# A 2-D Fourier transform with a channel mix: rows n and -n added on VectorE before the first products

## The chip, the core and the metric

The kernel runs on one core of one Trainium2 chip. The metric is device time in microseconds (us), the median over runs. The engines are named as in the profile: PE is TensorE with its weight loads (PEld), DVE is VectorE, ACT is ScalarE, POOL is GpSimd, SP is SyncE. PE writes only to PSUM; a result there is brought to SBUF by an "eviction" on ACT or DVE.

## What is computed

The input `x` is 8 x 3072 x 256 (batch, sequence, feature). The reference transforms both the sequence and the feature axis, keeps the real part, and feeds it to a channel mix:

```python
X = np.fft.fft(np.fft.fft(x, axis=1), axis=2).real
x_prev = np.concatenate([np.zeros((B, 1, D)), X[:, :-1, :]], axis=1)
xk = mu_k * X + (1.0 - mu_k) * x_prev
xr = mu_r * X + (1.0 - mu_r) * x_prev
k = np.maximum(xk @ w_k, 0.0)          # w_k: 256 x 1024
v = k * k @ w_v                        # w_v: 1024 x 256
out = v / (1.0 + np.exp(-(xr @ w_r)))  # w_r: 256 x 256
```

The input is real and only the real part is kept. So row n with feature f and row -n with feature -f (indices modulo 3072 and 256) enter with the same cosine. Their sum is all that the transform needs.

## The kernel before, in words

Each of the 8 batches goes through three product stages of the transform and then through the channel mix.

- **Loading.** `load_rows` (L105) brings 96 partitions of 16 rows into a tile `xh`, twice per batch (h = 0, 1). The upper 48 partitions hold the rows mirrored against the lower 48. The transfer is issued from POOL and turns float32 into float16.
- **Feature halves.** `butterfly` (L128) makes the sum and the difference of the two feature halves on DVE: four instructions of 96x2048 per batch, result `eo`.
- **Stage a.** `a_item` (L392): 8 products of 104 columns and one eviction of 128x832 on ACT, 8 items per batch. Where no `eo` is made (all of batch 0, half of batch 1) `a_sum` (L404) takes both feature halves as two accumulated products of 208 columns each, for 4 rows at a time.
- **Stage d.** `d_units` (L420), called by `d_item` and `d_half`: four products of 63 to 65 columns for each of 13 units; the eviction writes `g_all`. Its table is `w_eo`.
- **Stage c.** `c_item` (L446): two products of 64 columns for each of 27 slices, from `g_all` and the table `m_c` (for slice 0 also `mn`); the eviction writes `pq`. Then DVE forms `halves`, `diff` and the mixes (L466 to L526).
- **Channel mix.** 48 chunks of 512 rows, four steps each. `k_piece` (L543) is four products of 512 columns and a Relu eviction of 128x1024 on ACT, `square` (L552) squares on DVE, `v_tile` (L569) is 8 products of 256 columns, `r_item` (L557) is 8 products of 256 columns once per chunk, `v_out` (L580) scales on DVE and SP writes out.

**What sets the order.** Every engine runs its instructions in the order in which the program writes them; `pin_order` (L91) fixes that. The work of the transform for batch b+2 is put by hand at numbered steps of batch b with `at(step, function, ...)` (L626 to L727): kind "x" runs between `k_piece` and `v_tile`, kind "w" behind `v_tile`. Batch 0 runs ahead of step 0 (L598 to L620), batch 1 in steps 4 to 19. PSUM has three slots of 1024 columns (`ps_w`) and two of 512 (`ps_v`). `keep_busy` (L151) issues products with zeros that nobody reads.

**Tables at the start.** POOL fills index tables and, at L189 to L200, the angles `ueo` of the table `w_eo`. DVE wraps the angles at L272, ahead of the row tables (L284 to L295), of the angles of `m_c` (L341 and L342) and of everything that it does to batch 0:

```python
    ts(ueo, ueo, TURN - 1, ALU.bitwise_and)
    par_i = const.tile([P, 1], INT32)
    ts(par_i, pcol_i, 1, ALU.bitwise_and)
...
    m_angles(0, NJ1)
    m_wrap(0, NJ1)
```

`m_sine` (L328) turns the angles into the table on ACT, `m_first` (L334) mends its slice 0 with ACT and one DVE memset.

Of the kernel before, what the change touches and what calls it, by code (L numbers as in the profile page):

```python
# [9 lines left out]
FP32 = mybir.dt.float32  # L10
# [29 lines left out]
def kernel(  # L40
# [14 lines left out]
    P = 128  # L55
# [6 lines left out]
    xh_pool = ctx.enter_context(tc.tile_pool(name="xh", bufs=3))  # L62
# [39 lines left out]
    xh_t = {}  # L102
    eo_t = {}

    def load_rows(b, h, g, q0, nq):  # L105


        q = 16 * h + q0
        r = (64 - q if q else 32) if g else q
        src = dataclasses.replace(x[b, r:r + 1, :],  # L110
                                  ap=[[64 * D, N1], [-D if g else D, nq], [1, D]])
        nc.gpsimd.dma_start(out=xh_t[b, h][48 * g:48 * g + 48, q0:q0 + nq], in_=src)  # L112

    def load_part(b, h, q0, nq):
        load_rows(b, h, 0, q0, nq)
        if h == 0 and q0 == 0:
            load_rows(b, h, 1, 1, nq - 1)
            load_rows(b, h, 1, 0, 1)
        else:
            load_rows(b, h, 1, q0, nq)  # L120

    def load_xh(b, h):
        xh_t[b, h] = xh_pool.tile([96, 16, 256], FP16, name="xh")
        load_part(b, h, 0, 16)

    V = nc.vector

    def butterfly(b, h, e):  # L128
        if e == 0:
            eo_t[b, h] = eo_pool.tile([96, 16, 2, 128], FP16, name="eo")  # L130
        xh = xh_t[b, h]
        V.tensor_tensor(out=eo_t[b, h][:, :, e], in0=xh[:, :, 0:128], in1=xh[:, :, 128:256],  # L132
                        op=ALU.subtract if e else ALU.add)
# [46 lines left out]
    for h in range(2):  # L180
        xh_t[0, h] = xh_pool.tile([96, 16, 256], FP16, name="xh")
    load_rows(0, 0, 0, 0, 8)
# [4 lines left out]
    load_rows(0, 0, 1, 1, 7)  # L187
    load_rows(0, 0, 1, 0, 1)
# [9 lines left out]
    for c in range(2):  # L198
        nc.gpsimd.tensor_scalar(out=ueo[:, :, c], in0=veo_i[:, :, c], scalar1=pd_f,  # L199
                                scalar2=0.75 * (1 - c) * TURN, op0=ALU.mult, op1=ALU.add)  # L200
    load_part(0, 0, 8, 8)


    kst_i = const.tile([P, NJ + 64], INT32)
    nc.gpsimd.iota(kst_i[0:64, 0:NJ], pattern=[[2, NJ]], base=0, channel_multiplier=0)
    nc.gpsimd.iota(kst_i[64:128, 0:NJ], pattern=[[2, NJ]], base=-1, channel_multiplier=0)
    nc.gpsimd.iota(kst_i[:, NJ:NJ + 64], pattern=[[1, 64]], base=0, channel_multiplier=0)
    load_part(0, 1, 0, 8)
    load_part(0, 1, 8, 8)

# [9 lines left out]
    m_c = const.tile([P, 2 * NJ, 64], FP16)  # L220
    mn = const.tile([P, 64], FP16)
    V.memset(m_c, 0.0)
    V.memset(mn, 0.0)
# [20 lines left out]
    ts(one["p"], pcol_i, TURN / 48.0, MUL)  # L244
    ts(one["g"], pcol_i, 48.0, ALU.is_ge)
    ts(one["t"], one["p"], -2.0, MUL, 47.0 * TURN / 48.0, ADD)
    ts(one["n"], one["t"], one["g"], MUL, one["p"], ADD)
    ts(one["o0"], one["g"], 0.5 * TURN, MUL, 0.5 * TURN, ADD)
    ts(one["o1"], one["g"], 0.5 * TURN, MUL, 0.75 * TURN, ADD)
    for part, c, ph in ((0, 0, 0.75 * TURN), (0, 1, 0.0), (1, 0, one["o0"]), (1, 1, one["o1"])):  # L250
        ts(u_w[:, 0, part, :, c], k1c_i, one["n"], MUL, ph, ADD)
    ts(one["ph"], one["p"], TURN / 96.0, ADD)
    ts(one["a"], pcol_f, 48.0, ALU.is_lt, one["p"], MUL)
    ts(one["b"], pcol_f, 48.0, ALU.is_ge, one["ph"], MUL)
    ts(one["fa"], one["g"], -0.25 * TURN, MUL, 0.75 * TURN, ADD)
    ts(one["fb"], one["g"], 0.25 * TURN, MUL, 0.5 * TURN, ADD)
    for part, c, by, ph in ((0, 0, "a", one["fa"]), (0, 1, "b", one["fb"]),
                            (1, 0, "a", 0.5 * TURN), (1, 1, "b", 0.5 * TURN)):
        ts(u_w[:, 1, part, :, c], k1c_i, one[by], MUL, ph, ADD)
    u_f = u_w.rearrange("p t a k c -> p (t a k c)")  # L260
    ts(u_f, u_f, TURN - 1, ALU.bitwise_and)
    nc.scalar.activation(out=w_pm[:, :, 0:2],
                         in_=_v(u_f, 0, [(4 * NU, 2), (0, 2), (1, 4 * NU)]), func=AF.Sin,
                         bias=m_pi, scale=TWO_PI / TURN)
    nc.scalar.activation(out=w_pm[:, :, 2], in_=_v(u_f, 0, [(4 * NU, 2), (1, 4 * NU)]),
                         func=AF.Sin, bias=p_pi, scale=-TWO_PI / TURN)

    for i in range(2):
# [11 lines left out]
    ast = const.tile([P, NJ + 64], FP32)  # L280
    ast_i = const.tile([P, 64], INT32)
    row = {n: const.tile([P, 1], FP32, name=f"row_{n}")
           for n in ("s", "c", "rr", "rs", "ph0", "ph", "sgn")}
# [3 lines left out]
    ts(row["rr"], t64_i, row["c"], ADD, row["s"], ADD)  # L287
    ts(row["rs"], t64_i, row["c"], ADD, float(TURN) / S, MUL)
    ts(row["ph0"], row["c"], 0.25 / 32 * TURN, MUL, 0.75 * TURN, ADD)
    ts(row["ph"], row["s"], 0.25 / 32 * TURN, MUL, row["ph0"], ADD)  # L290
    ts(row["sgn"], row["s"], 1.0 / 16, MUL, -1.0, ADD)
    ts(ast_i, kst_i[:, NJ:NJ + 64], row["rr"], MUL, float(TURN) / R, MUL)
    ts(ast_i, ast_i, TURN - 1, ALU.bitwise_and)
    V.tensor_copy(out=ast[:, NJ:NJ + 64], in_=ast_i)
    ts(ast[:, 0:NJ], kst_i[:, 0:NJ], row["rs"], MUL, row["ph"], ADD)  # L295
# [3 lines left out]
    def rows():  # L299
# [17 lines left out]
           .rearrange("p a b -> p (a b)").bitcast(INT32)[:, 0:NJ * 64]  # L317
           .rearrange("p (s t) -> p s t", t=64))
    lo64, hi64 = slice(0, 64), slice(64, 128)

    def m_angles(j0, j1):
        V.tensor_tensor(out=ang[:, j0:j1], in0=_v(ast, j0, [(1, j1 - j0), (0, 64)]),
                        in1=_v(ast, NJ, [(0, j1 - j0), (1, 64)]), op=ALU.add)

    def m_wrap(j0, j1):
        ts(ang[:, j0:j1], ang[:, j0:j1], TURN - 1, ALU.bitwise_and)

    def m_sine(j0, j1):  # L328
        for part, odd in ((hi64, 0), (lo64, 1)):
            nc.scalar.activation(  # L330
                out=m_c.rearrange("p (j o) t -> p j o t", o=2)[part, j0:j1, odd],
                in_=ang[part, j0:j1], func=AF.Sin, bias=m_pi[part], scale=TWO_PI / TURN)

    def m_first():  # L334

        im = slice(96, 128)
        nc.scalar.activation(out=m_c[im, 0], in_=m_c[im, 0], func=AF.Copy, scale=row["sgn"][im])
        V.memset(m_c[hi64, 0, 0:1], 0.0)
        nc.scalar.activation(out=mn[hi64], in_=m_c[hi64, 0], func=AF.Copy, scale=-1.0)

    m_angles(0, NJ1)  # L341
    m_wrap(0, NJ1)  # L342

    def gather(dst, w, n):
        nc.gpsimd.indirect_dma_start(dst, None, w,
                                     bass.IndirectOffsetOnAxis(ap=row_i[:, n:n + 1], axis=0))

    xh_t[1, 0] = xh_pool.tile([96, 16, 256], FP16, name="xh")

    def loads():  # L350
        load_part(1, 0, 0, 8)
        for a in range(2):
            next(row_part)
            gather(wk_sb[0][a], moe_w_k, a)
        nc.gpsimd.dma_start(out=wv_sb, in_=moe_w_v.rearrange("(fc p) v -> p fc v", p=128))
        load_part(1, 0, 8, 8)
        for a in range(2):
            gather(wr_sb[0][a], moe_w_r, a)
# [30 lines left out]
    def a_tile(b):  # L389
        a_t[b] = y_pool.tile([P, 2, 2, NU, 64], FP16, name="a")  # L390

    def a_item(b, h, e, j, eng="A"):  # L392

        if (h, e, j) == (0, 0, 0):
            a_tile(b)
        eo = eo_t[b, h]
        ps = ps_w()
        for i in range(8):
            nc.tensor.matmul(out=ps[:, 128 * i:128 * i + 4 * NU], lhsT=eo[:, 8 * j + i, e, :],  # L399
                             rhs=w_pm[0:96, int(h + j + i == 0), 0], start=True, stop=True)  # L400
        evac(_v(a_t[b], 128 * NU * e + 16 * h + 8 * j, [(32, 4 * NU), (1, 8)]),
             _v(ps, 0, [(1, 4 * NU), (128, 8)]), eng)

    def a_sum(b, h, q0, eng="A", n=4):  # L404
# [4 lines left out]
        xh = xh_t[b, h]  # L409
        ps = ps_w() if n == 4 else ps_v()  # L410
        for i in range(n):
            for k in range(2):
                nc.tensor.matmul(out=ps[:, 256 * i:256 * i + 8 * NU],  # L413
                                 lhsT=xh[:, q0 + i, 128 * k:128 * k + 128],
                                 rhs=w_pm[0:96, int(h + q0 + i == 0), k:k + 2],
                                 start=(k == 0), stop=(k == 1))
        evac(_v(a_t[b], 16 * h + q0, [(32, 8 * NU), (1, n)]),
             _v(ps, 0, [(1, 8 * NU), (256, n)]), eng)
# [360 lines left out]
```

## Time and profile before

| | us |
|---|---|
| median of 3 runs (453.25 to 454.44) | 453.86 |
| span of the profiled execution, first to last instruction | 450.4 |
| PE busy in the span | 439.9 |
| DVE busy | 352.6 |
| ACT busy | 345.0 |
| POOL busy | 43.5 |

The profiled execution has a span of 450.4 us; no total of its own is recorded beside it, and the median of the runs lies 3.46 us above the span.

How to read it: a timeline line gives the start in us, the duration in us, the engine, the source line, the operation, what it writes and reads, and how many instructions are merged (x16). Durations of PE products contain their way through the array and overlap, so the cost of a product in a stream is taken from start to start of neighbouring groups. A row of windows gives, after the stretch and its length, the busy time of PE, PEld, DVE, ACT and POOL with the instructions of each, then the granted TensorE clock as a share of full speed, the DMA share and GB/s. A group row gives the count, the total and the mean ns of one.

### The profile page before, as it was taken

To read this page: it belongs to the slowest core of one execution; us is meant where nothing else is said; L and a number is where in the kernel's file an instruction comes from. 1 tells how busy PE (TensorE), PEld (TensorE's weight loads), DVE (VectorE), ACT (ScalarE), POOL (GpSimd) and SP (SyncE) were. 2 spreads that over 40 slices of the span, in tenths; PEclk is the share of its full clock that TensorE was granted. 3 is DMA by queue.
4 is the path that set the end of the run, shared out by engine and by line. 5 is a ranking of instruction groups with operands and counts; after the bars stand their busy time and mean duration, and the time that the engine had idled before them with its cause. 6 is when DMAs were issued, how large, how long until landed. Compare 5 with 4: busy or idle time off the path is not lost.

```text
span 450.4 us, 9677 instructions
## 1 busy us (share of the span) xinstructions
PE 439.9 (98%) x4073; PEld 321.4 (71%) x4073; DVE 352.6 (78%) x472; ACT 345.0 (77%) x390; POOL 43.5 (10%) x78
## 2 busy tenths in 40 slices
PE   7899999999999999999999999999999999999996
PEld 4667777777777777777777777777777777676764
DVE  6599969986788878977789877888779755997453
ACT  6599898787878778877888778887778787666661
POOL 8862010102000110001100010000000000000000
PEclk8799999999999999999999999999999999999999
DMA  7997961737622385225923272222323232233333
GB/s 103 159 201 109 180 119 47 141 71 129 131 49 69 60 158 109 54 60 98 172 48 71 51 137 67 53 66 54 72 48 72 47 71 58 61 71 71 72 70 95
DMA packets 43856, 40.22 MB, mean 89 GB/s; under 512 B 3986, under 2 KB 42388, under 8 KB 43188
## 3 DMA queue, kind: packets, MB, share of 16 engines
q1 hardware_dynamic: 27524, 25.05, 22.7%
q0 software_dynamic: 16128, 14.42, 22.5%
q8 instruction: 32, 0.52, 0.5%
q10 hardware_dynamic: 160, 0.13, 0.1%
q14 instruction: 12, 0.10, 0.1%
HBM read 28.84 MB, written 25.17 MB: 120 GB/s over the span
## 4 chain that ended last, share of the span: by engine, by line
PE 93%; ACT 2%; POOL 1%; DMA 1%; DVE 1%; issue 0%; POOLq 0%
PE psV L576 37%; PE psW L538 36%; PE psW L562 9%; PE psW L399 4%; PE psW L457 3%; PE psW L427 2%; PE psW L413 1%; ACT rl L548 1%; DMA xh<-in_x_dram 1%; POOL xh L112 1%; ACT L567 0%; PE psV L413 0%; ACT r L567 0%; DVE y L474 0%; POOL ueo L199 0%
## 5 line engine op out<-in xcount | busy, mean ns | idle before, releaser
L548 ACT ACTIVATE rl<-psW 128x1024 f16<-128x1024 f32 x192 | 196.2, 1024 | 87.7 <-PE psW L538 87.5
L576 PE MATMUL psV<-wv_sb,k 128*128 128x256 f16 x1536 | 198.7, 272 | 0.0
L538 PE MATMUL psW<-x,wk 128*128 128x512 f16 (+1 forms) x776 | 196.7, 377 | 0.8 <-DVE x L518 0.5
L555 DVE TENSOR_TENSOR k<-rl 128x2048 f16<-128x2048 f16 (+1 forms) x98 | 117.5, 1202 | 60.7 <-ACT rl L548 60.0
L576 PEld LDWEIGHTS <-k 128*128 128x128 f16 x1536 | 143.6, 98 | 23.0 <-DVE k L555 0.2
L538 PEld LDWEIGHTS <-wk 128*128 128x128 f16 x776 | 75.8, 98 | 50.9 <-issue 1.3
L586 DVE SCALAR_TENSOR_TENSOR o<-psV,r 128x512 f32<-128x512 f32 (+1 forms) x97 | 66.1, 683 | 20.8 <-PE psV L576 19.2
L507 DVE TENSOR_TENSOR x<-y,t 128x1536 f16<-128x1536 f16 x60 | 57.5, 959 | 2.1
L387 ACT ACTIVATE a<-psW 128x832 f16<-128x832 f32 x61 | 52.3, 859 | 3.6 <-PE psW L413 3.6
L562 PE MATMUL psW<-wr,x 128*128 128x256 f16 x384 | 49.8, 273 | 0.0
L567 ACT ACTIVATE r<-psW 128x1024 f16<-128x1024 f32 x48 | 48.9, 1018 | 0.8 <-PE psW L562 0.8
L112 POOL DMA_DIRECT2D xh<-in_x_dram x46 | 28.7, 632 | 215.2 <-DVE eo L132 214.3
L562 PEld LDWEIGHTS <-x 128*128 128x128 f16 x384 | 37.6, 98 | 14.4
L399 PEld LDWEIGHTS <-eo 96*128 96x128 f16 x416 | 24.4, 97 | 11.6
L132 DVE TENSOR_TENSOR eo<-xh 96x2048 f16<-96x2048 f16 x26 | 31.5, 1214 | 0.0
L387 ACT ACTIVATE pq<-psW 128x896 f16<-128x896 f32 (+5 forms) x34 | 28.5, 845 | 1.1 <-PE psW L457 1.1
L399 PE MATMUL psW<-w_pm,eo 96*128 96x104 f16 x416 | 27.6, 209 | 0.0
L387 ACT ACTIVATE g_all<-psW 128x1024 f16<-128x1024 f32 (+1 forms) x31 | 26.4, 857 | 0.0
L457 PEld LDWEIGHTS <-g_all 128*128 128x128 f16 x432 | 16.8, 98 | 8.5 <-ACT g_all L387 2.3
L427 PEld LDWEIGHTS <-a 128*128 128x128 f16 x416 | 16.6, 97 | 7.2 <-issue 0.4
L494 DVE TENSOR_SCALAR t<-d,mu_m 128x1536 f16<-128x1536 f16 x32 | 19.7, 614 | 0.0
L474 DVE TENSOR_TENSOR y<-pq 128x896 f16<-128x896 f16 (+5 forms) x38 | 18.6, 532 | 1.0 <-ACT pq L387 0.7
(100 smaller groups left out, 154.7 us busy)
## 6 DMA issues: line engine op xcount, KB each, us to landing
out_dram<-o SPq DMA_DIRECT2D x190, 128.0 KB, 2.4
xh<-in_x_dram POOLq DMA_DIRECT2D x20, 384.0 KB, 6.5
xh<-in_x_dram POOLq DMA_DIRECT2D x6, 360.0 KB, 7.8
xh<-in_x_dram POOLq DMA_DIRECT2D x10, 192.0 KB, 5.3
wv_sb<-in_moe_w_v_dram POOLq DMA_DIRECT2D x1, 512.0 KB, 8.7
xh<-in_x_dram POOLq DMA_DIRECT2D x2, 168.0 KB, 5.4
xh<-in_x_dram POOLq DMA_DIRECT2D x8, 24.0 KB, 6.5
out_dram<-o ACTq DMA_DIRECT2D x2, 64.0 KB, 2.1
```

Of the source, the lines that this page charges most:

```text
L112: nc.gpsimd.dma_start(out=xh_t[b, h][48 * g:48 * g + 48, q0:q0 + nq], in_=src)
L132: V.tensor_tensor(out=eo_t[b, h][:, :, e], in0=xh[:, :, 0:128], in1=xh[:, :, 128:256], op=ALU.subtract if e else ALU.add)
L387: nc.scalar.activation(out=out_ap, in_=in_ap, func=AF.Copy)
L399: nc.tensor.matmul(out=ps[:, 128 * i:128 * i + 4 * NU], lhsT=eo[:, 8 * j + i, e, :], rhs=w_pm[0:96, int(h + j + i == 0), 0], start=True, s ...
L507: V.tensor_tensor(out=dst, in0=_v(y_t[b], 64 * (NSL * a + lo + 3 * m), [(1, n)]), in1=_v(x_t["t", a], 64 * lo, [(1, n)]), op=ALU.subtract ...
L538: nc.tensor.matmul(out=st["k", ds][:, 512 * hs + lo:512 * hs + hi], lhsT=wk_sb[m][a][:, 128 * fc:128 * fc + 128], rhs=xk[:, a, 512 * i + l ...
L548: nc.scalar.activation(out=st["rl"][:, 2 * ds:2 * ds + 2], in_=st["k", ds].rearrange("p (f t) -> p f t", f=2), func=AF.Relu, bias=0.0, sca ...
L555: V.tensor_tensor(out=k2_t[c][:, lo:hi], in0=r, in1=r, op=ALU.mult)
L562: nc.tensor.matmul(out=ps[:, 256 * tb:256 * tb + 256], lhsT=x_t[b, 1, m][:, a, 512 * i + 128 * tb: 512 * i + 128 * tb + 128], rhs=wr_sb[m] ...
L567: nc.scalar.activation(out=st["r", c], in_=ps, func=AF.Sigmoid)
L576: nc.tensor.matmul(out=st["v", tb - h][:, 256 * h:256 * h + 256], lhsT=k2_t[c][:, fc, 128 * tb:128 * tb + 128], rhs=wv_sb[:, fc], start=(f ...
L586: V.scalar_tensor_tensor(out=o.rearrange("p a b -> p (a b)")[:, 0:256 * n], in0=st["v", t0][:, 0:256 * n], scalar=16.0, in1=st["r", c][:, ...
```

## The change

Per batch only half of the rows go into stage a: `fold` adds row n and row -n on DVE, the second with its feature index running backwards. The rows n are loaded by direct transfers (`load_p`) to `xp`, the rows -n by indirect transfers with an index per partition (`load_m`) to `xm`, both from POOL. `butterfly` and the products of stage a then take half as many rows. Stage d has two products of 128 columns per unit in place of four, stage c 28 products per batch (26 of them 128 columns wide) in place of 54, with two tables `m_cs`. A product of 13 columns with a table `turn` (`turned`) and its eviction correct one column group of `g_all` ahead of stage c; in the first 17 slices of batch 0 a third product per cut (`turn_late`) does this instead. At the start the loads of batch 0 become ten issues on POOL, and the filling of `veo_i`, `pd_f` and `ueo` moves behind them. Behind `ueo` POOL fills `idx_8`. L272 stays where it is on DVE; behind it the 7 entries of the row tables become 19, and `ast` has two rows of angles. `turn_table` is six instructions on DVE. In `a_item` two products of 52 columns replace one of 104 in the second half. The steps of the transform's items are set anew.

```diff
+    def load_p(b, h, q0, n):
+        r = 0 if q0 == 8 else 8 * h + q0 + 1
+        src = dataclasses.replace(x[b, r:r + 1, :], ap=[[32 * D, 96], [D, n], [1, D]])
+        nc.gpsimd.dma_start(out=xp_t[b, h][:, q0:q0 + n], in_=src)
+    def gather(dst, src, idx):
+        nc.gpsimd.indirect_dma_start(dst, None, src, bass.IndirectOffsetOnAxis(ap=idx, axis=0))
+    def load_m(b, h, q0, n):
...
+        gather(xm_t[b, h][:, o:o + 256 * n], x.rearrange("b (s r) d -> (b s) (r d)", r=n), idx)
+    def fold(b, h, q0=0, n=0):
+        n = n or 8 + h
...
+        o = XM0 + 1792 - 256 * q0
+        V.tensor_tensor(out=p[:, q0:q0 + n], in0=xp[:, q0:q0 + n],
+                        in1=_v(xm, o + 256, [(-256, n), (-1, 256)]), op=ALU.add)
+        V.tensor_tensor(out=p[:, q0:q0 + n, 0], in0=xp[:, q0:q0 + n, 0],
+                        in1=_v(xm, o, [(-256, n)]), op=ALU.add)
+    def butterfly(b, h):
+        n = 8 + h
...
+        for e in range(2):
+            V.tensor_tensor(out=eo_t[b, h][:, 0:n, e], in0=p[:, 0:n, 0:128],
+                            in1=p[:, 0:n, 128:256], op=ALU.subtract if e else ALU.add)
...
+    load_p(0, 0, 0, 4)
     pcol_i = const.tile([P, 1], INT32)
     nc.gpsimd.iota(pcol_i, pattern=[[0, 1]], base=0, channel_multiplier=1)
+    nc.gpsimd.iota(idx_4, pattern=[[-1, 4]], base=S // 4 - 1, channel_multiplier=-8)
...
+    load_m(0, 0, 0, 4)
+    load_p(0, 0, 4, 4)
+    load_m(0, 0, 4, 4)
...
+    load_p(0, 1, 0, 4)
+    load_m(0, 1, 0, 4)
+    load_p(0, 1, 8, 1)
+    load_m(0, 1, 8, 1)
+    load_p(0, 1, 4, 4)
+    load_m(0, 1, 4, 4)
     veo_i = const.tile([P, 2, 2, 64], INT32)
...
-    ts(row["s"], t64_i, 32.0, ALU.is_equal, 32.0, MUL)
...
+    def turn_table():
...
     def m_angles(j0, j1):
-        V.tensor_tensor(out=ang[:, j0:j1], ...
+        V.tensor_tensor(out=ang[:, :, j0:j1], ...
     def m_first():
+        nc.scalar.activation(out=m_cs[im, 0, 0], ...
+        nc.scalar.activation(out=m_cs[hi64, 1, 0], ...
+        V.memset(m_cs[hi64, :, 0, 0:1], 0.0)
     def a_item(b, h, e, eng="A"):
...
+            if h and i == 7:
+                for q, o, w in ((8, 0, _v(w_pm[0:96], WA, [(1, WB)])),
+                                (7, 1, _v(w_pm[0:96], 0, [(2, WB)]))):
...
     def d_units(b, ps, u0, n, bank):
-            for e, part, c0, c1 in ((0, 0, 0, 65), (0, 1, 65, 128), (1, 0, 0, 64), (1, 1, 64, 128)):
+            for e in range(2):
+    def turned(u0, u1):
+        ps = ps_w()
+        f128 = _v(g_all, 256 * u0 + 128, [(256, u1 - u0)])
+        nc.tensor.matmul(out=ps[:, 0:u1 - u0], lhsT=turn, rhs=f128, start=True, stop=True)
+        evac(f128, ps[:, 0:u1 - u0], "A")
+    def c_item(b, s0, n, eng="A", turn_late=False):
...
+        cuts = [s0] + list(range(s0 + 1 + s0 % 2, s0 + n, 2))
+        for f in range(3 if turn_late else 2):
+            for sl in cuts:
+                k = min(1 + sl % 2, s0 + n - sl)
...
-    loads()
+    fold(0, 0, 0, 4)
+    a_sum(0, 0, 0)
     eo_sine()
     eo_rest()
-    a_sum(0, 0, 0)
+    m_angles(0, NJ1)
+    fold(0, 0, 4, 4)
     a_sum(0, 0, 4)
-    keep_busy(1)
+    m_wrap(0, NJ1)
+    fold(0, 1, 0, 4)
+    a_sum(0, 1, 0)
     m_sine(0, NJ1)
     m_first()
+    fold(0, 1, 4, 5)
+    loads()
+    a_sum(0, 1, 4, "V", 2)
+    a_sum(0, 1, 6, "A", 2)
+    mu_turn()
...
-    c_item(0, 0, 5)
-    c_item(0, 5, 4)
+    c_item(0, 0, 5, "A", True)
+    c_item(0, 5, 4, "A", True)
...
+    at(2, turn_table)
+    at(5, turned, 8, 13)
     at(5, c_item, 0, 17, 8)
+    at(4, fold, 1, 0)
     at(5, a_sum, 1, 0, 0)
-    at(6, butterfly, 1, 1, 0)
-    at(6, butterfly, 1, 1, 1)
+    at(6, fold, 1, 1)
     at(7, a_sum, 1, 0, 4)
+    at(7, butterfly, 1, 1)
...
             for n, st0 in enumerate((9, 10, 12, 14) if b else (13, 15, 16, 24)):
-                at(s0 + st0, butterfly, t, n // 2, n % 2)
+                at(s0 + st0, butterfly if n % 2 else fold, t, n // 2)
+            for n, st0 in enumerate((18, 21, 23, 25) if b else (18, 21, 25, 26)):
+                at(s0 + st0, a_item, t, n // 2, n % 2)
+            for n, st0 in enumerate((27, 29, 31, 33)):
+                at(s0 + st0, d_item, t, n)
+            at(s0 + 34, turned, 0, 13)
+            for n, st0 in enumerate((35, 37, 39, 41)):
+                at(s0 + st0, c_item, t, (0, 7, 15, 21)[n], (7, 8, 6, 6)[n])
```

More of the change, by code (lines that the diff above doesn't have):

```diff
@@ L99 @@
     first_inst = len(list(nc.cur_bb.bb.instructions))
[L102 to L118, printed above, removed]
-        else:
-            load_rows(b, h, 1, q0, nq)
+    xp_t, xm_t, p_t, eo_t = {}, {}, {}, {}
@@ L124, in load_xh @@
[L124 to L133, printed above, removed]
+        x_tiles(b, h)
+        for q0, n in ((0, 8), (8, 1))[:1 + h]:
+            load_p(b, h, q0, n)
+            load_m(b, h, q0, n)
+    def fold(b, h, q0=0, n=0):
+        n = n or 8 + h
+        if (b, h) not in p_t:
+            p_t[b, h] = p_pool.tile([96, 9, 256], FP16, name="p")
+        p, xp, xm = p_t[b, h], xp_t[b, h], xm_t[b, h]
+        o = XM0 + 1792 - 256 * q0
[3 more added lines that the diff above has]
+                        in1=_v(xm, o, [(-256, n)]), op=ALU.add)
@@ L217 @@
     g_all = const.tile([P, NU // 2, 256], FP16)
[L220 to L223, printed above, removed]
+    m_cs = const.tile([P, 2, 2 * NJ, 64], FP16)
+    V.memset(m_cs, 0.0)
     warm = const.tile([P, 1], FP32)
@@ L260 @@
[L260 to L263, printed above, removed]
+    ts(g_i, pcol_i, 1, ALU.bitwise_and)
+    ts(one["h"], pcol_i, TURN / 96.0, MUL)
+    ts(one["n"], g_i, -TURN / 96.0, MUL, one["h"], ADD)
+    ts(one["n1"], g_i, one["n"], MUL)
+    ts(one["n0"], one["n1"], -1.0, MUL, one["n"], ADD)
+    ts(one["n2"], g_i, one["h"], MUL)
@@ new lines @@
+    for n, lo, hi in (("f0", 0.75, 0.5), ("f1", 0.5, 0.75), ("f2", 0.625, 0.5), ("f3", 0.5, 0.625)):
+        ts(one[n], g_i, (hi - lo) * TURN, MUL, lo * TURN, ADD)
+    for o, step, by, ph in ((0, 4, "n0", one["f0"]), (1, 4, "n1", one["f1"]),
+                            (2, 4, "n0", 0.5 * TURN), (3, 4, "n1", 0.5 * TURN),
+                            (WA, 2, "n0", one["f2"]), (WA + 1, 2, "n2", one["f3"])):
+        ts(_v(u_w, o, [(step, NU)]), k1c_i, one[by], MUL, ph, ADD)
+    ts(u_w, u_w, TURN - 1, ALU.bitwise_and)
@@ L626, in at @@
     def at(step, f, *args):
-        work.setdefault((step, "x" if f in (a_item, a_sum, d_item, c_item, r_item, m_sine) else "w"),
+        work.setdefault((step, "x" if f in (a_item, a_sum, d_item, c_item, turned, r_item, m_sine) else "w"),
                         []).append((f, args))
@@ L692 @@
     at(14, mix, 0, 1, 1, 1)
[L693 to L695 removed]
+    for n, st0 in enumerate((9, 10)):
+        at(st0, a_item, 1, 1, n, "A")
+    for n, st0 in enumerate((11, 12, 13, 14)):
         at(st0, d_item, 1, n)
[L697 to L698 removed]
+    at(15, turned, 0, 13)
+    for n, st0 in enumerate((16, 17, 18, 19)):
+        at(st0, c_item, 1, (0, 7, 15, 21)[n], (7, 8, 6, 6)[n])
     for b in range(B):
```

234 lines of the change are left out of this document (118 added, 116 removed).

## The prediction

> **What bounds the kernel now.** I read first the busy time by stretches of the span (stretch, length, busy PE, PEld, DVE, ACT, POOL, granted clock, DMA share, GB/s).
>
> ```profile
> 10.00:15.00 5.00, 4.82 (x29) 3.94 (x27) 2.35 (x4) 2.77 (x5) 3.71 (x10) 0.50 1.19 184
> 50.00:60.00 10.00, 10.00 (x123) 7.62 (x122) 9.92 (x12) 9.16 (x11) 1.29 (x2) 1.00 0.63 113
> 207.00:260.50 53.50, 53.50 (x520) 39.39 (x517) 43.49 (x52) 42.74 (x47) 3.11 (x5) 1.00 0.46 90
> ```
>
> From 50 us on PE has no gap: what PE saves there comes off the time while the others keep up. DVE and ACT have 10 us to spare per 53.5 us later on, but at 50 to 60 us DVE has none. At 10 to 15 us PE runs at clock 0.50. Then the timeline of PE, for the price of a product as start-to-start.
>
> ```profile
> 170.16 1.03 PE L538 MATMUL psW<-x,wk 128*128 128x512 f16 x4
> 171.03 0.53 PE L399 MATMUL psW<-w_pm,eo 96*128 96x104 f16 x8
> 171.40 1.04 PE L576 MATMUL psV<-wv_sb,k 128*128 128x256 f16 x8
> ```
> ```profile
> 206.63 0.64 PE L427 MATMUL psW<-w_eo,a 128*128 128x65 f16 x16
> 207.11 1.04 PE L576 MATMUL psV<-wv_sb,k 128*128 128x256 f16 x8
> ...
> 213.19 0.57 PE L457 MATMUL psW<-m_c,g_all 128*128 128x64 f16 x14
> 213.60 1.04 PE L576 MATMUL psV<-wv_sb,k 128*128 128x256 f16 x8
> ```
>
> Eight products of 104 columns take 0.37 us, 46 ns each; 16 of 64 take 0.48, 14 take 0.41: 29.5 ns. So a column costs 0.41 ns and a product about 3 ns besides. Merging products saves only these 3 ns; halving columns saves much.
>
> Last the start, where the change moves most.
>
> ```profile
> 3.92 0.24 POOL L196 TENSOR_SCALAR pd_f<-pcol_i 128x1 f32<-128x1 int32 x1
> 4.26 0.74 POOL L199 TENSOR_SCALAR ueo<-veo_i,pd_f 128x128 int32<-128x128 int32 x2
> 4.95 1.26 POOL L112 DMA_DIRECT2D xh<-in_x_dram  x2
> ...
> 18.77 1.02 POOL L345 DMA_INDIRECT wr<-in_moe_w_r_dram,row_i  x1 [0.30 <-issue]
> 20.10 1.03 POOL L345 DMA_INDIRECT wr<-in_moe_w_r_dram,row_i  x1 [0.30 <-issue]
> ```
> ```profile
> 5.26 0.38 DVE L240 TENSOR_SCALAR ueo<-ueo 128x256 int32<-128x256 int32 x1
> ...
> 7.99 0.76 DVE L322 TENSOR_TENSOR rl<-ast 128x576 int32<-128x576 f32 x1
> 8.78 0.62 DVE L240 TENSOR_SCALAR rl<-rl 128x576 int32<-128x576 int32 x1
> ```
>
> POOL does one thing at a time: a direct issue holds it 0.63 us, an indirect one 1.33 with its gap. DVE wraps `ueo` at 5.26, right behind POOL; the 14 instructions from there to 7.99 take 2.73 us.
>
> **Steady batches (2 to 7).** Stage a: 64 x 46 ns = 2.95 us becomes 30 x 46 + 4 x 30 = 1.50, a gain of 1.45. Stage d: 52 x 29.5 = 1.53 becomes 26 x 56 (128 columns x 0.41 + 3) = 1.46, gain 0.07. Stage c: 54 x 29.5 = 1.59 becomes 26 x 56 + 2 x 29.5 = 1.52, gain 0.07. `turned` adds 0.03. Together -1.56 per batch, six times: **-9.4 us**. The eviction of `turned` sits behind one Relu eviction (1.02) on ACT, and the next step's stage c is 1.75 us away (two groups of 0.87): no stall. ACT drops 4 evictions of 0.86 per batch and gains some 0.2. DVE loses four `butterfly` of 1.21 and gains four of 0.69 to 0.75 (from the 128x1024 form, 0.69) and two folds of about 1.3, each with a small second instruction of 0.1 to 0.2: 43.5 becomes about 44.4 of 51.9 us. Both fit.
>
> **Batch 1.** `a_sum` there: 16 fewer products at 90 ns (8 took 0.72 in the chain of waits at 31.67), -1.44; its `a_item` half -0.72; d and c -0.11: **-2.3 us**.
>
> **The start.** Ten issues now come ahead of `ueo` on POOL, and L272 stands on DVE ahead of the row tables and every fold. POOL: first issue at 1.24, five direct at 0.63, five indirect at 1.35, eight iotas at about 0.2, then `veo` 0.48, `pd_f` and `ueo` 1.08: `ueo` is done near 14.4 us (5.0 now). DVE then has 27 small instructions where 14 took 2.73; taking dependent ones at 0.18 and independent at 0.07, as in that stretch, 4.8 us: the first fold starts near 19.2, though its rows landed long before. From there one chain: fold 0.8, angles 1.3 (twice 576 elements, from 0.76 and the 0.57 of 320), fold 0.8, wrap 1.3, fold 0.8, `a_sum` 1.6 at half clock, eviction 0.9, two sines of 1.25 (0.77 for 576 elements, 0.56 for 320), `m_first` 0.65, the memset on DVE, for which the last fold behind it must wait, 0.1, fold 0.95, `a_sum` 1.6, eviction 0.55: 33.1 us. Now stage d starts at 18.65, which is 4.9 us ahead of the first products of the mix (23.55). With the third product of `turn_late` and half clock I take 5.4: 38.5 in place of 23.55, **+15.0 us**. The loads of weights and of batch 1 come 12 us later than now or less, still ahead of their use.
>
> **Early steps.** (1) Clock. Now PE falls to 0.50 near 7.5 us and is back near 17.5, after 8 us with hardly a gap. In the new start PE works a quarter of the time from 20 to 33 us, so the mix begins cold: **+2** (nothing if warm, 4 if the first 28 products, 10240 columns, all run at half clock: 8.5 for 4.8 us). The Trainium skill, "TensorE: Matmul & The Clock Gate", Part 1, has full clock back after some 3.4 us of steady work; by that figure the term would be nearer 1.5 (an estimate). The stretch above speaks for longer. (2) In step 5 `turned` and the stage c that reads it are neighbours: PE waits for a Relu eviction and a short one, **+1.0** (0.5 to 1.5). (3) DVE, which has no gap from 36 to 60 us, gets `turn_table` (1.1) and for batch 1 two folds and a `butterfly` (4.2) for 2.4 now: 3 us more, while PE needs 2.3 less. DVE's backlog can run some 3 us behind before `v_tile` feels it: **+1.5** (0 to 4).
>
> The fold's second source runs backwards from an odd element, and no row shows such a read. Nearest are the mixes of L507: half of them write backwards from an odd element, and all 60 take 957 to 961 ns. So I take the fast rate (1.21 for 2048); the other end is one element per ns, from the scalar_tensor_tensor forms (0.74 for 512, 0.48 for 256), 2.3 us. The Trainium skill, "VectorE: DVE Perf Modes", section "Mode 2×_1P", asks for step 1 or -1 and 4-byte alignment; its alignment would speak against this change (2.1 us a fold, an estimate), and L507, which breaks it, shows no loss.
>
> **Sum.** 450.4 + 15.0 + 2.0 + 1.0 + 1.5 - 9.4 - 2.3 = 458.2 us of span. The median lies 3.46 above the span now; kept so: **461.6 us**. Ends: the start is +11.2 if an indirect issue costs what a direct one does, and +18.6 at the longest indirect issue (1.39) with slow folds; all terms at their good ends give 454.2, all at their bad ends about 470.
>
> **Rivals.**
> - *Faster: the folds begin when their rows land.* If DVE reaches the first fold near 10 us (loads landed, row tables done), not 19.2, the start loses 9.1 and 1 us of cold clock: 451.5. That needs `ueo` ready early, so POOL's order or L272 other than written; engines keep the written order in the trace, which speaks against it. It decides from a first fold before about 11 us. Chance 0.14.
> - *Indirect issues are cheap* (fewer partitions than the 128 of L345): 458 us. For it: 0.94 was seen once. Chance 0.16.
> - *Slow folds.* The four of the start cost 1.9 more in sum, batches 1 and 2 some 2 us on a DVE without gaps: 465.5. Later DVE has room. L507 speaks against. Chance 0.17.
> - Forecast, 459 to 464: 0.53.
>
> The kernel is faster only in the first rival: by more than 0.3% (about what a measurement of this kernel can tell from no change; 1.4 us) 0.13, within it 0.07, slower 0.80. The range 453 to 468 leaves out the first rival and the worst ends.
>
> **What would show it.** Right: DVE idle until about 14 us for POOL's `ueo`; first fold at 18 to 20; first products of the mix at 37 to 40; clock 0.50 into the mix; period of a batch from 53.0 to 51.4; folds of 1.2 to 1.3 us. Wrong: a first fold near 10, a period that stays at 53, PE gaps at stage c in later batches, or a gap on POOL from DMA.

## The result, and the profile after

The changed kernel takes **459.76 us** (median of 4 runs, 459.53 to 460.61) against 454.06 us for the kernel before in the same session (453.25 to 454.44): 1.0132 times as long, 95% interval 1.0116 to 1.0148. Forecast were 461.6 us and a range of 453 to 468. The profiled execution took 459.53 us; its span is 457.8 us, 7.4 more than before. So the products saved did come off, and the start took more than that back. Two runs of the kernel before, beside c_after and e9 to e11 below, took 769.03 and 1626.32 us and are left out of all figures.

The later part first: a stretch of ten us and one whole batch period by the windows of the changed kernel (columns as in the windows of before: stretch, length, PE, PEld, DVE, ACT, POOL, clock, DMA share, GB/s).

```profile
50.00:60.00 10.00, 9.97 (x85) 7.36 (x83) 9.90 (x16) 9.26 (x11) 6.88 (x6) 1.00 0.76 105
201.40:252.88 51.48, 51.48 (x427) 37.41 (x425) 43.60 (x56) 39.34 (x44) 4.97 (x6) 1.00 0.46 95
```

PE is still without a gap through a whole batch, and does it with 427 products, where the 53.5 us of before held 520. The period is 51.48 us, from 53.01 before (between the same products of two batches): 1.53 us less per batch. DVE's busy time stays what it was (43.5 in the 53.5 us of before), ACT has 3.4 us less.

The price is in the timeline of the start of the changed kernel:

```profile
12.47 0.72 POOL L241 TENSOR_SCALAR ueo<-veo_i,pd_f 128x128 int32<-128x128 int32 x2
13.23 0.29 DVE L276 TENSOR_SCALAR ueo<-ueo 128x256 int32<-128x256 int32 x1 [7.55 <-POOL ueo L241]
...
17.89 0.68 DVE L148 TENSOR_TENSOR p<-xp,xm 96x1024 f16<-96x1024 f16 x1
...
18.84 1.57 PE L475 MATMUL psW<-w_pm,p 96*128 96x208 f16 x8 [13.41 <-DVE p L150]
...
28.17 0.06 DVE L400 MEMSET m_cs<- 64x2 f16 x1 [5.86 <-DMA wv_sb<-in_moe_w_v_dram]
28.31 0.82 DVE L148 TENSOR_TENSOR p<-xp,xm 96x1280 f16<-96x1280 f16 x1
...
32.19 1.03 PE L490 MATMUL psV<-w_eo,a 128*128 128x128 f16 x8
37.45 1.02 ACT L438 ACTIVATE g_all<-psW 128x1024 f16<-128x1024 f32 x1 [1.41 <-PE psW L490]
39.59 2.78 PE L608 MATMUL psW<-x,wk 128*128 128x256 f16 x20
```

Two idle times of DVE carry the start: 7.55 us at L276 (the line that was L272), until POOL has filled `ueo` behind ten DMA issues, and 5.86 us at L400, the memset of `m_first`, behind which the last fold stands. PE waits 13.41 us for the first fold. The first products of the mix come at 39.59 us; before it was 23.55. The trace puts the memset's wait down to the load of `wv_sb`; three experiments below put the same wait down to ACT's `m_cs` (L398), which ends in the same tenth of a microsecond.

How much each stretch moved, by the same products in both traces:

| shift against before, us | predicted | measured |
|---|---|---|
| first products of the mix | +15.0 | +16.04 |
| from there to the first `r_item` product | +2.0 +1.0 +1.5, less part of batch 1's gain | +2.24 |
| batch 1 (first to fourth `r_item`) | -2.3 | -2.63 |
| from there to the end (steady batches) | -9.4 | -8.3 |
| sum (span) | +7.8 | +7.4 |

### The profile page after: what moved, and what is told of

Read it like the earlier page. It is cut to its first block, busy times and chain, and to the rows that moved or that the text cites. A ratio compares the mean times of both kernels' runs of the same rounds, so it can differ in the third digit from the quotient of the medians.

```text
span 457.8 us, 8433 instructions
## 1 busy us (share of the span) xinstructions
PE 428.6 (94%) x3433; PEld 307.2 (67%) x3433; DVE 363.2 (79%) x523; ACT 325.1 (71%) x369; POOL 61.9 (14%) x88
## 4 chain that ended last, share of the span: by engine, by line
PE 85%; DVE 6%; POOL 4%; issue 1%; DMA 1%; ACT 1%; POOLq 0%; DVEq 0%
PE psV L646 35%; PE psW L608 33%; PE psW L632 9%; PE psW L528 3%; PE psW L490 3%; PE psW L458 2%; DVE k L625 2%; DMA wv_sb<-in_moe_w_v_dram 1%; POOL xm L124 1%; DVE x L588 1%; DVE d L552 1%; DVE p L148 1%; POOL xp L121 1%; DVE o L656 0%; POOL wk L124 0%
## 5 line engine op out<-in xcount | busy, mean ns | idle before, releaser
L121 POOL DMA_DIRECT2D xp<-in_x_dram x26 | 15.1, 580 | 200.5 <-DVE p L150 187.8
L438 ACT ACTIVATE a<-psW 128x832 f16<-128x832 f32 x31 | 26.6, 859 | 14.0 <-PE psW L475 14.0
L124 POOL DMA_INDIRECT xm<-in_x_dram,idx x26 | 30.9, 1187 | 7.8 <-issue 7.6
L438 ACT ACTIVATE pq<-psW 128x768 f16<-128x768 f32 (+5 forms) x34 | 28.6, 844 | 2.5 <-PE psW L528 2.3
L438 ACT ACTIVATE g_all<-psW 128x1024 f16<-128x1024 f32 (+3 forms) x39 | 28.1, 723 | 1.4 <-PE psW L490 1.4
L528 PEld LDWEIGHTS <-g_all 128*128 128x128 f16 (+1 forms) x233 | 15.2, 99 | 11.5 <-ACT g_all L438 3.3
L528 PE MATMUL psW<-m_cs,g_all 128*128 128x128 f16 (+2 forms) x233 | 19.2, 222 | 2.5 <-ACT g_all L438 2.3
L544 DVE TENSOR_TENSOR y<-pq 128x960 f16<-128x960 f16 (+5 forms) x38 | 18.6, 531 | 3.2 <-ACT pq L438 1.9
L148 DVE TENSOR_TENSOR p<-xp,xm 96x2048 f16<-96x2048 f16 (+3 forms) x18 | 20.8, 1155 | 0.1
L475 PEld LDWEIGHTS <-p 96*128 96x128 f16 x50 | 5.9, 130 | 22.1 <-DVE p L150 21.4
```

The costliest lines, as they stand in the source:

```text
L124: nc.gpsimd.indirect_dma_start(dst, None, src, bass.IndirectOffsetOnAxis(ap=idx, axis=0))
L148: V.tensor_tensor(out=p[:, q0:q0 + n], in0=xp[:, q0:q0 + n], in1=_v(xm, o + 256, [(-256, n), (-1, 256)]), op=ALU.add)
L438: nc.scalar.activation(out=out_ap, in_=in_ap, func=AF.Copy)
L528: nc.tensor.matmul(out=ps[0:m, o:o + 64 * k], lhsT=g_all[:, u, 128 * min(f, 1):128 * min(f, 1) + m], rhs=m_cs[:, f % 2, sl:sl + k], start= ...
```

## The experiments

**Theory:** PE sets the time from the mix on, so each product saved comes off; the start loses more because DVE stands at L276 for `ueo`, and again at L400 for ACT, while rows that have landed wait. **Rivals:** the indirect loads of the mirrored rows land late; the fold is slow; the cold clock, not the order, makes the start long; `turned` makes PE wait.

The table gives all runs; each stands beside runs of the kernel before on the same chip. Differences between experiments are taken from the changed kernel run again ("c_after", 458.40), on another chip than e1 to e8. The start of the mix in the traces, against 38.53 us in c_after, gives nearly the same for e1 (-6.85), e2 (-7.64) and e3 (-3.23), and -7.75 for e7; for e4 it gives only -1.30, its profiled run being the longest of its six. The ratio is the recorded one and not the quotient of the two medians. None of these kernels leaves out part of the computation; where products are added, nobody reads them or they are written twice to one place.

| run | us (median) | before, same chip | ratio, 95% interval | less c_after |
|---|---|---|---|---|
| c_after | 458.40 | 452.40 | 1.0142 (1.0106 to 1.0178) | |
| e1_wrap_late | 451.42 | 452.68 | 0.998 (0.9962 to 0.9997) | -6.98 |
| e2_ueo_first | 450.83 | 452.68 | 0.9957 (0.9939 to 0.9974) | -7.57 |
| e3_fold_first | 455.25 | 452.68 | 1.0057 (1.0041 to 1.0073) | -3.15 |
| e4_warm | 456.34 | 452.68 | 1.0094 (1.0065 to 1.0123) | -2.06 |
| e5_narrow | 459.43 | 453.53 | 1.0136 (1.0095 to 1.0178) | +1.03 |
| e6_a_twice | 466.91 | 453.53 | 1.0302 (1.0259 to 1.0345) | +8.51 |
| e7_start | 449.86 | 453.53 | 0.9923 (0.9899 to 0.9947) | -8.54 |
| e8_start_no5 | 449.42 | 453.53 | 0.9929 (0.99 to 0.9958) | -8.98 |
| e9_order | 449.44 | 452.40 | 0.9933 (0.9914 to 0.9952) | -8.96 |
| e10_order_warm | 446.80 | 452.40 | 0.9889 (0.9852 to 0.9927) | -11.60 |
| e11_no5 | 458.58 | 452.40 | 1.0146 (1.011 to 1.0182) | +0.18 |

### The wait for `ueo`, from both ends (e1, e2)

e1 leaves POOL alone and moves DVE's instruction behind the folds that it held up:

```diff
-    ts(ueo, ueo, TURN - 1, ALU.bitwise_and)
...
-    eo_sine()
-    eo_rest()
     m_angles(0, NJ1)
...
     m_wrap(0, NJ1)
+    ts(ueo, ueo, TURN - 1, ALU.bitwise_and)
     fold(0, 1, 0, 4)
...
     m_first()
+    eo_sine()
+    eo_rest()
```

Expected: 

> The changed kernel with the wrap of ueo on VectorE (and the sines that read it) moved behind the angles and the wrap of m_cs; GpSimd's order is untouched. Theory (VectorE stood idle from 5.7 to 13.2 us for GpSimd's ueo, and the whole start hangs behind it): first fold near 10.4 us instead of 17.9, stage d near 24.7 instead of 32.2, the median falls by 7 to 8 us, to about 452. Rival (the loads of batch 0 are what the start waits for, the last indirect one is issued only at 10.8 us): the folds begin earlier but the last one still waits for its rows, and the gain is under 3 us.

e2 leaves DVE alone and moves POOL's block (the filling of `veo_i`, `pd_f` and `ueo`, lines unchanged) ahead of eight of the ten issues:

```diff
     load_m(0, 0, 0, 4)
+    veo_i = const.tile([P, 2, 2, 64], INT32)
...
     load_p(0, 0, 4, 4)
...
     load_m(0, 1, 4, 4)
-    veo_i = const.tile([P, 2, 2, 64], INT32)
...
```

Expected: 

> The changed kernel with GpSimd's work on veo, pd and ueo put back ahead of eight of the ten x loads; VectorE's order is untouched. Theory: the wait of 7.5 us goes, the loads come 1.5 us later, first fold near 10.4 us, median 452 to 453, the same as when the wrap itself is moved. Rival (loads decide): the later loads eat the gain, 457 or more, and this kernel is slower than the one with the wrap moved by the 1.5 us of GpSimd's work.

Measured: 451.42 and 450.83 us. In e1 the first fold starts at 10.03 us and stage d at 25.33. The timeline of e2:

```profile
5.64 0.22 DVE L276 TENSOR_SCALAR ueo<-ueo 128x256 int32<-128x256 int32 x1
...
10.23 0.68 DVE L148 TENSOR_TENSOR p<-xp,xm 96x1024 f16<-96x1024 f16 x1
...
20.51 0.06 DVE L400 MEMSET m_cs<- 64x2 f16 x1 [5.86 <-ACT m_cs L398]
...
21.09 0.99 POOL L407 DMA_DIRECT2D wv_sb<-in_moe_w_v_dram  x1
```

The wrap and the fold come 7.6 us earlier, and the whole kernel gets 7.57 us faster: none of it is lost on the way. Two edits on two engines that share only this wait give the same 7 to 7.6 us, so the wait is the cause. The rows had landed by 10 us, so for the first fold the rival of late indirect loads falls. With either edit the sign of the change turns, though by little: e2 is 0.4% faster than before, e1 0.2%, which is less than the 0.3% that the prediction takes such a measurement to tell. The memset's wait is the same 5.86 us as in the changed kernel, with all its neighbours 7.6 us earlier, and now the releaser named is ACT. In e2 the load of `wv_sb` is issued only at 21.09 us, behind the memset (in e1 at 21.40, behind 21.30), so it can't be what the memset waits for.

### The second wait: the last fold behind the memset (e3)

```diff
     a_sum(0, 1, 0)
+    fold(0, 1, 4, 5)
     m_sine(0, NJ1)
     m_first()
-    fold(0, 1, 4, 5)
     loads()
```

Expected: 

> The changed kernel with the last fold of batch 0 put ahead of the memset that mends slice 0 of m_cs, so that it no longer waits for the sines on ScalarE. Theory (the memset waited for ScalarE's sines and the fold stood behind it, 5.9 us of idle VectorE; the trace names the wv_sb transfer only because it ended in the same moment): stage d starts near 26.5 us, stage c near 29 when the sines are done, median 4 to 5 us lower, about 455. Rival (the wait is for the wv_sb transfer or for rows that land late): no change, within 0.5 us.

Measured: 455.25 us, 3.15 faster, less than the 4 to 5 expected. The timeline of e3:

```profile
22.30 0.82 DVE L148 TENSOR_TENSOR p<-xp,xm 96x1280 f16<-96x1280 f16 x1
...
28.14 0.06 DVE L400 MEMSET m_cs<- 64x2 f16 x1 [4.82 <-ACT m_cs L398]
...
28.97 1.01 PE L490 MATMUL psV<-w_eo,a 128*128 128x128 f16 x8 [2.38 <-DVE a L436]
```

The fold comes 6.0 us earlier, stage d only 3.2. The memset stands where it was, at 28.1, and the evictions of stage a that follow it on DVE, or follow the sines on ACT, now hold stage d. What the fold gains beyond 3.2 us is given back to the next instruction behind the same wait.

### The clock of the start (e4), and the changed kernel again (c_after)

e4 keeps PE busy with products of zeros, from 1 us to the first `a_sum`, and once more behind the third:

```diff
-    keep_busy(10)
+    keep_busy(66)
...
     a_sum(0, 1, 0)
+    keep_busy(12)
     m_sine(0, NJ1)
```

Expected of e4: 

> The changed kernel with products of zeros that nobody reads put into TensorE's two long gaps of the start (66 instead of 10 at the beginning, 12 behind the third a_sum). Theory (the products of the start run at half clock although the granted-clock rows of the profile say 1.00: 8 products of 128 columns take 0.97 us at stage d): each a_sum 0.7 us shorter, stages d and c about half, stage d to the first products of the mix 5 us instead of 7.4, median 3 to 4 us lower, about 456. Rival (the clock was full, what stretches the start is waits between the engines): no change, or slower where the zeros stand in the way.

Expected of c_after (no edit): 

> The changed kernel once more, unaltered, as the measure for the others on one chip. Its first profile has 1.06 us between stage d of units 4 to 7 and its eviction on ScalarE (37.45 us, where 36.40 was due) that the kernels with the split and the doubled products do not have, although their start is the same. If that belongs to the kernel, the median is 459.8 again and the gap is there; if it was that placement or that chip, it is near 458.7.

The windows of c_after show the granted clock (third column from the right) in the start:

```profile
10.00:15.00 5.00, 0.00 (x0) 0.00 (x0) 1.56 (x11) 0.00 (x0) 4.29 (x10) 0.50 0.95 134
...
30.00:35.00 5.00, 4.74 (x33) 3.46 (x31) 2.60 (x5) 1.56 (x3) 3.58 (x6) 0.50 1.10 202
37.00:38.00 1.00, 0.63 (x7) 0.32 (x7) 0.96 (x3) 0.41 (x1) 1.00 (x1) 1.00 1.05 135
```

PE has nothing to do at 10 to 15 us and the clock is at half. At 30 to 35 us PE works 4.74 of 5 us and still has half the clock; at 37 us it has all of it. The timeline of c_after goes on:

```profile
36.39 1.02 ACT L438 ACTIVATE g_all<-psW 128x1024 f16<-128x1024 f32 x1 [0.37 <-PE psW L490]
...
38.53 2.78 PE L608 MATMUL psW<-x,wk 128*128 128x256 f16 x20
```

The mix begins with full clock: 20 products with 6144 columns in 2.78 us, 0.45 ns a column. In this execution it begins at 38.53 us, +14.98 on before. The first profile of the changed kernel had 1.06 us more between stage d and this eviction (37.45 against 36.39); e5, e6 and e11 do not have it either. It is no property of the kernel, and its cause stays open. It went whole into the time: from there to the end each `r_item` of the first profile lies 1.06 us later than in c_after. That first profile's clock column reads 1.00 in the start, though its 8 products of 208 columns took 1.57 us as at half clock; the spacing of the products decides there, not the column.

e4 took 456.34 us, 2.06 faster, where 3 to 4 were expected. Its timeline:

```profile
18.84 0.89 PE L475 MATMUL psW<-w_pm,p 96*128 96x208 f16 x8 [1.50 <-DVE p L150]
...
22.37 1.57 PE L475 MATMUL psW<-w_pm,p 96*128 96x208 f16 x8 [0.58 <-DVE p L150]
...
31.10 0.62 PE L490 MATMUL psV<-w_eo,a 128*128 128x128 f16 x8
```

The first `a_sum` takes 0.89 us for 1.57, and stage d's group 0.62 for 1.03. But the third `a_sum`, at 22.37 us, took 1.57 again after gaps of 1.50, 1.18 and 0.58 us: only part of the start was warm. By the windows of e4 the clock went to 0.50 at 22.0 us and was back at 25.4, 3.0 us after the products had begun again, the zeros running from 23.73; that is much sooner than in c_after. The cold clock costs 1.3 us (start of the mix) to 2.1 us (medians) here, and the wait alone 7; the clock is the smaller part, not the cause.

### Products saved and products merged (e5, e6)

e5 splits each 128-column product of stages d and c into two of 64, e6 issues each 104-column product of stage a twice into the same place:

```diff
-                nc.tensor.matmul(out=ps[:, o:o + 128],
...
+                for c in (0, 64):
+                    nc.tensor.matmul(out=ps[:, o + c:o + c + 64],
...
```
```diff
+                for _ in range(2):
                     nc.tensor.matmul(out=ps[:, 128 * i:128 * i + WA], lhsT=eo[:, i, e, :],
```

Expected of e5: 

> The changed kernel with every 128-column product of stages d and c split into two of 64 columns with the same weights; columns, evictions and results stay. Theory (a product costs its columns and 3 ns besides): 52 more products per batch, 0.16 us per batch, about 1.3 us over 8 batches, median near 461. Rival (the weight load that each product brings shows up, the load of 98 ns not being hidden behind 27 ns of columns): 10 us or more.

Expected of e6: 

> The changed kernel with each 104-column product of the stage-a items issued twice into the same place, with the same result; 30 more products per batch for batches 2 to 7 and 14 for batch 1, no other engine gets work. Theory (TensorE is the bound without a gap, so halving the columns of stage a paid its full price): 194 products more at 46 ns, 8.9 us, median near 468.6, a batch from 51.5 to 52.9 us. Rival (part of what stage a saved was not on the path, VectorE or ScalarE being late anyway): 5 us or less.

Measured: 459.43 us (+1.03) and 466.91 us (+8.51). The timeline of PE in e5:

```profile
151.57 0.63 PE L491 MATMUL psW<-w_eo,a 128*128 128x64 f16 x16
152.03 1.04 PE L648 MATMUL psV<-wv_sb,k 128*128 128x256 f16 x8
```

Start to start, 16 products of 64 columns take 0.46 us; in the changed kernel 8 of 128 take 0.45. So the wider products are worth 0.13 us a batch (51.61 against 51.48), about 1 us over eight batches (an estimate). The period is the evidence for this, not the +1.03, which compares two chips and of which 0.44 us lie ahead of the mix (38.97 against 38.53). The rival of a visible weight load, 10 us or more, falls. In e6 the period grows to 52.85, by 1.37 us, which is 30 times 46 ns: stage a's products are paid in full, and halving them is where the saving is.

### `turned` in step 5 (e11)

```diff
-    at(5, turned, 8, 13)
-    at(5, c_item, 0, 17, 8)
+    at(5, c_item, 0, 17, 8, "A", True)
...
-    at(8, c_item, 0, 25, 2)
+    at(8, c_item, 0, 25, 2, "A", True)
```

Expected: 

> The changed kernel with only the turned of step 5 taken out (the third product per cut does its work for the last ten slices of batch 0). Theory: TensorE's 0.95 us wait at stage c in step 5 goes, 0.8 us lower than the changed kernel on this chip. Rival (VectorE is late in these steps anyway): no difference beyond 0.3 us.

Measured: 458.58 us, +0.18: nothing. In the changed kernel (c_after, timeline) PE does stand still between `turned` and stage c:

```profile
48.50 0.40 PE L528 MATMUL psW<-m_cs,g_all 128*128 128x128 f16 x4 [0.95 <-ACT g_all L438]
48.73 0.88 PE L475 MATMUL psW<-w_pm,p 96*128 96x208 f16 x8
```

Without `turned`, in the timeline of e11:

```profile
47.15 0.92 PE L528 MATMUL psW<-m_cs,g_all 128*128 128x128 f16 x12
48.74 0.89 PE L475 MATMUL psW<-w_pm,p 96*128 96x208 f16 x8 [0.67 <-DVE p L150]
```

The 0.95 us are gone, and the next `a_sum` starts at 48.74 for 48.73: it waits for its fold on DVE. The stall was hidden behind another.

### A better start (e7 to e10)

e7 puts e2 and e3 together, gives the second late eviction of stage a and the first of stage d to DVE, and takes the memset out of `m_first` and puts it behind them. e8 is e7 with the edit of e11. The edit of e7 without the block of e2:

```diff
     a_sum(0, 1, 0)
+    fold(0, 1, 4, 5)
     m_sine(0, NJ1)
     m_first()
-    fold(0, 1, 4, 5)
...
-    a_sum(0, 1, 6, "A", 2)
+    a_sum(0, 1, 6, "V", 2)
...
-    d_half(0, 0, ps_v(), "A")
+    d_half(0, 0, ps_v(), "V")
     d_half(0, 2, ps_v(), "V")
+    V.memset(m_cs[hi64, :, 0, 0:1], 0.0)
```

Expected of e7: 

> The changed kernel with its start mended in three places: GpSimd's ueo back ahead of eight of the ten loads, the last fold ahead of the sines, and the last evictions of stages a and d of batch 0 on VectorE with the memset of m_cs behind them. Theory (the three delays lie one after the other on one chain: 8.9, 4.5 and about 1.9 us): median near 444.5, under the kernel before by about 8 us. Rival (with the first two gone the rows of the last loads or the sines decide): the parts do not add up, 447 or more.

Expected of e8: 

> The same start as in the kernel with the three repairs, and in addition no turned in step 5: the third product per cut does its work for the last ten slices of batch 0 as well. Theory (in step 5 TensorE waits 0.95 us for ScalarE's Relu and the short eviction): 0.8 us lower than that kernel. Rival (VectorE is behind in these steps and the wait only shows up elsewhere): no difference.

Measured: 449.86 us (448.73 to 450.88) and 449.42 (448.79 to 451.12). e7's theory fell: only 1 us better than e2, where 6 were hoped for. The timeline of e7 says why:

```profile
19.10 0.86 DVE L148 TENSOR_TENSOR p<-xp,xm 96x1280 f16<-96x1280 f16 x1 [4.45 <-DMA xm<-in_x_dram,idx]
...
25.39 1.89 PE L527 MATMUL psW<-m_cs,g_all 128*128 128x64 f16 x15 [1.34 <-DVE m_cs L687]
```

Here the rival of late loads is true: once DVE is early, the last mirrored rows are late. Their issue is the tenth on POOL, and e2's block ahead of it pushes it back (12.59 us for 10.75 in c_after). What was still gained there was given back at stage c, which waits 1.34 us for the memset that now stands behind DVE's evictions: the mix begins at 30.78 us, 0.11 earlier than in e2. In e8, with the same start, the last fold begins at 17.79 us, 1.31 earlier, so the landing of these rows differs from one execution to the next. e7 and e8 overlap, so e8 by itself settles nothing on `turned`.

e9 therefore leaves POOL's loads first, as the change has them, and orders DVE around them: the wrap behind the third fold, the sines of `m_c` ahead of the third eviction, that eviction on DVE, the memset (out of `m_first`) ahead of the last fold, the second half of the angles behind stage d, and the edit of e11. e10 adds zero products to e9: `keep_busy(10)` at the start becomes 38, and `keep_busy(11)` stands behind the third `a_sum`. The edit of e9 without its later parts:

```diff
-    ts(ueo, ueo, TURN - 1, ALU.bitwise_and)
...
     fold(0, 1, 0, 4)
-    a_sum(0, 1, 0)
     m_sine(0, NJ1)
     m_first()
+    a_sum(0, 1, 0, "V")
+    ts(ueo, ueo, TURN - 1, ALU.bitwise_and)
+    eo_sine()
+    eo_rest()
+    V.memset(m_cs[hi64, :, 0, 0:1], 0.0)
     fold(0, 1, 4, 5)
```

Expected of e9: 

> The changed kernel with loads first on GpSimd (as in the change), the wrap of ueo behind the third fold, the sines of m_cs ahead of the third eviction on ScalarE, that eviction on VectorE, the memset just ahead of the last fold, the second angles behind stage d, and no turned in step 5. Theory (what is left of the start is the last load, which lands near 17.6 us, and then fold, a_sum, eviction): stage d near 21.5 to 22.5 us, first products of the mix near 28, median near 447.5. Rival (VectorE's own chain is as long): no gain over the kernel with three repairs, 449.5 or more.

Expected of e10: 

> The same order, with zero products in TensorE's gaps (38 at the beginning, 11 behind the third a_sum). Theory (half clock costs a_sum, d and c): a further 2 to 2.5 us, near 445; at half clock one such product is 0.43 us, at full 0.22. Rival (loads hide it, the gaps grow by what the products save): within 0.5 us of the kernel without zeros.

Measured: 449.44 us (449.10 to 449.72) and 446.80 us (446.18 to 447.44). e9 missed its 447.5 by 2 us, and e10 its 445. The timeline of e9:

```profile
18.89 0.06 DVE L679 MEMSET m_cs<- 64x2 f16 x1 [1.50 <-ACT m_cs L397]
19.03 0.82 DVE L148 TENSOR_TENSOR p<-xp,xm 96x1280 f16<-96x1280 f16 x1
```

The last fold starts at 19.03 us, behind the memset, which waited 1.50 us for ACT's `m_first`. That is the time that e9's rival named, but not its reason: DVE waits for ACT, its own chain is not as long. The zero products are worth 2.64 us in the medians; in the traces the mix begins 3.61 us earlier (26.18 for 29.79). The timeline of e10:

```profile
18.20 0.06 DVE L680 MEMSET m_cs<- 64x2 f16 x1 [0.82 <-ACT m_cs L397]
...
21.14 0.62 PE L488 MATMUL psV<-w_eo,a 128*128 128x128 f16 x8
26.18 1.01 PE L606 MATMUL psW<-x,wk 128*128 128x256 f16 x7
```

The mix begins at 26.18 us, 2.6 later than before and 12.4 earlier than in c_after. e10 is **1.1% faster than the kernel before** (0.9852 to 0.9927), with the folds, the tables and the wider products of the change kept. Without the added zeros e9 is 0.7% faster (0.9914 to 0.9952). The kernel before has a stretch at clock 0.50 too, and whether zeros there would make it faster was not tried, so only e9's part can be put down to the change and its order: the idea pays once its start is in order.

## Why the prediction was right, step by step

- **The start, +15.0: right in size, +14.98 in c_after, by the steps named.** `ueo` was done at 13.19 us (14.4 forecast), since direct issues held POOL 0.55 to 0.70 and indirect ones 0.93 to 0.97, with a gap of 0.30 before all but the first. From the wrap to the first fold it took 4.66 us (4.8). The fold started at 17.89 (19.2), stage d at 32.19 (33.1). What was 1 us early there was given back before the mix at half clock: 6.36 us from stage d to the mix, 5.4 taken. The first profile has +16.04, and its 1.06 us more were in no term. e1 and e2 show the first wait and e3 the second.
- **The clock, +2 in the mix: wrong, it measured 0.** The mix is warm (20 products in 2.78 us), and the sign "clock 0.50 into the mix" did not come; the half clock sits inside the start, where the terms of the +15.0 had it already. The Trainium skill, "TensorE: Matmul & The Clock Gate", Part 1, has the full clock back after some 3.4 us of steady work. The traces of e4 and e10 agree (3.0 and 3.3 us, with a stream of zeros); in c_after it took 7.5 (from 29.4 to 36.9 us) and in the trace of before 8.1 (from 9.5 to 17.6), with other products. Why they differ stays open.
- **`turned` +1.0 and DVE's backlog +1.5: not a sum.** The gap is there (0.95), the fold is late by 0.67 without it, and one hides the other (e11). With the cold start of the mix (0) and batch 1's first part, the stretch cost 2.24 in all, where the three terms had 4.5.
- **Batch 1, -2.3: right** (-2.63).
- **Steady batches, -9.4: right in kind, a little high.** Per batch 1.53 came off (1.56 forecast), and from batch 1's end to the last instruction 8.3. Counted in stretches of six chunks from the fourth `r_item` on, the first gave 0.67 and each of the next five 1.53. In the first, PE stands still for 0.47 us at 92.9 (it waits for a mix `x` on DVE); the rest of what is missing there is not traced. e6 and e5 confirm both prices: 46 ns for a product of 104 columns; 2.5 ns saved per product merged (3 forecast).
- **The folds: fast, as taken.** The groups by form of the changed kernel:

```profile
L148 DVE TENSOR_TENSOR p<-xp,xm 96x2304 f16<-96x2304 f16 x7 | 9.4, 1348 | 0.0
L148 DVE TENSOR_TENSOR p<-xp,xm 96x2048 f16<-96x2048 f16 x7 | 8.5, 1212 | 0.0
```

  1212 ns for 2048 elements, 0.59 ns each, is the rate of the old `butterfly` (1.21 us). The rival of slow folds falls. The rule of 4-byte alignment in the Trainium skill, "VectorE: DVE Perf Modes", section "Mode 2×_1P", is not put to the test by this read, and the prediction was wrong to take it as one that breaks the rule. The read runs backwards from element 2305 of its tile, so its neighbours 2305 and 2304 lie in one 4-byte word, counted from the start of the tile; the writes of L507 (1535 and 1534) are of the same kind. What the runs do show is that running backwards costs nothing.
- **The median above the span, 3.46: a mis-sized term, 1.7 of the 1.84 us missed.** Where a run has both numbers, time and span lie 1.7 to 1.9 us apart (459.53 and 457.8; for a run of before 452.39 and 450.6). So the profiled execution of before took about 452.2 us (an estimate from these two), and was itself 1.7 us under the median: runs of the kernel before spread from 450.57 to 454.44. 458.2 of span and 1.75 give 459.95; the profiled run took 459.53. That the span came so close is partly luck: the 1.06 us that were in no term made up for terms that were too dear. By c_after, without them, the span grew by 6.3 us where +7.8 was forecast.
- **The rivals.** "Folds begin when their rows land" was priced at 451.5 us; e1 and e2 built its condition, first fold at 10.0 to 10.2, and took 451.42 and 450.83. Cheap indirect issues (458) came in a small part: 0.08 us an issue. The good ends of the sum are slightly misadded: 450.4 + 11.2 + 0.5 - 9.4 - 2.3 + 3.46 is 453.9, not 454.2, and five indirect issues at 0.63 in place of 1.35 make the start +11.4, not +11.2.

## What to carry to other kernels

Every engine runs in written order, so a small preparation step written ahead of the main chain (here one wrap of 0.3 us) costs the whole wait of its slowest producer; before DMA issues are added on an engine, look for what is written behind them and who waits for it. A saving on the bounding engine is paid once per batch, a delay of the start once per launch: price both, and reorder the start before giving up the idea. When a wait is removed, ask what is waited for next: e3 got less than expected because the evictions stood behind the same sines, e7 because the last rows were late and the memset then held stage c, and e11 got nothing.

## What the runs showed of the hardware

- The clock of PE came back 7.3 to 9.5 us after the products had begun again in before, c_after, e1, e2 and e9, whose streams have short gaps, but after 3.0 (e4) and 3.3 us (e10) where zero products followed each other; what decides is open. In e4 gaps of 1.50, 1.18 and 0.58 us took it away (8 products of 208 columns 0.89 us, then 1.57), in e10 gaps of 1.18 and 0.58. Products of zeros from 1 us on kept it until then, and in all were worth 2.06 (e4) and 2.64 us (e10) in the medians.
- The kernel before spreads over 3.7 us beside e1 to e4, and the mean granted clock leans the same way (450.57 us at 0.998, 454.32 at 0.984), but not in every run (453.24 at 0.995). e2 and c_after spread over only 0.4 us. Why they do not share that spread is open.
- A weight load per product is hidden even at 64 columns: twice as many products of half the width cost 2.5 ns each.
- A releaser can be named wrongly when two events end together (L400, 5.86 us: the load of `wv_sb` in the changed kernel, ACT in e2 for the same 5.86 us, in e1 for 5.85), and a clock column can be without its record; the spacing of products showed the clock then.
